# Six check reductions, one tile's split and six small additions change their place in a fused attention and two-layer kernel

## The chip, the cores and the metric

One core of a Trainium2 chip runs the whole program. The engines are the tensor engine (PE in the profile; PEld are its weight loads), VectorE (DVE), ScalarE (ACT), GpSimd (POOL) and SyncE (SP, here only an issuer of DMAs). The time is the device time of one execution in microseconds; the number compared is the median of several executions.

## The reference

Three stages follow one another. The first is attention with 4 batches, 8 heads, 768 positions and heads of 64, in which each position sees the first `n_global` positions and the `n_local` last ones, with a bias that falls with the distance:

```
scores = scale * q @ k.T - slope[h] * dist       # kept where global or local, else -1e9
a = exp(scores - max);  a = a / (sum(a) + 1e-9)
x = (a @ v), as 3072 rows of 512
h = x @ w_in;  x2 = (h * sigmoid(h)) @ w_out     # 512 -> 2048 -> 512
logits = x2 @ phi                                # 32 slots
d = softmax over the rows;  slot_input = d.T @ x2
slot_out[e] = relu(slot_input[e] @ w1[e]) @ w2[e]
out = softmax over the slots(logits) @ slot_out
```

## The kernel before

The 3072 rows are 24 tiles of 128 (six for each batch, `TPB`), and the tiles make 8 chunks of three. Everything lies in one hand-laid arena in SBUF, so most operands in the profile are called `arena`; PSUM is eight banks.

*Attention.* For each tile T: `load` brings q, k and v (for tiles 6 and up into the staging buffers `stage_m`, so that the next load waits until the tile before has been split), `split` makes a high and a low half in 16 bits (`hi`, L200, L202 or L204 by engine, and `lo`, L208 or L210), `s_step` computes the scores of two heads (matmuls L317 or L327, then on VectorE L332 adds the bias and takes the extreme, on ScalarE L333 takes the exponential and adds up the row sums into `psum_`), and `pv_step` multiplies by v (matmuls L372) and divides by the row sums: an addition of 1e-9 (L383), a reciprocal (L384) and the scaling of the rows (L385). The tiles 0 to 5 are called paired: their q and k are used as they are loaded.

*The two layers.* For each chunk `l1_step(c, f)` runs 12 matmuls (L504 to L506) for each of 16 blocks of 128 columns, then the gating: tanh on ScalarE (L508), a product on VectorE (L510, its instruction is appended to the list `gated`), the high half on ScalarE (L200) and the low half on VectorE (L210). Its outputs rotate through four banks. `l2_part` and `l2_end` do the second layer (L524 to L526) and its output's halves, which SyncE transposes (L537).

*The weights.* They arrive as 16 parts of 64-bit words and are converted in the kernel by `conv`: an unpacking on ScalarE (L462), a mask on VectorE (L464), a check of the masked bits by two matmuls (L469), a shift on VectorE (L472), the high half on ScalarE (L482) and the low half, the second part, on VectorE (L490). Part p's L490 must be done before the second layer's matmuls that use its low half. Parts 8 to 15 are those of the second layer; the last of them are converted during the second layer of the first chunk.

*The checks.* `absmax` (L213) takes the largest magnitude of a sample of some halves, and L895 the largest of the odd bits found by the weight checks; all of them are looked at near the end of the kernel, where a flag decides whether a slower program runs.

*The order.* The text interleaves: while a chunk runs through its layers, the attention items of the next chunks are called between the steps, so many a step, in a list made by `other_items`. What each engine executes is ordered afterwards by a scheduler that goes by its own estimate of when an instruction's operands are ready; the order of the text is its preference. `tc.issue_after(ins)` makes the instructions of its block on the engine of `ins` queue behind `ins`.

Of the kernel before, what the change touches and what calls it, by code (L numbers as in the profile page):

```python
# [12 lines left out]
ALU = mybir.AluOpType  # L13
AX = mybir.AxisListType
# [18 lines left out]
CHUNKS = [3, 3, 3, 3, 3, 3, 3, 3]  # L33
# [12 lines left out]
def p2(e):  # L46
    return float(2.0 ** e)
# [53 lines left out]
def fast_kernel(tc, keepp, q_l, k_l, v_l, q_f, k_f, n_global, n_local, w_in, w_out, phi, w1, w2, shapes, pick_c, out):  # L101
# [8 lines left out]
    with ExitStack() as ctx:  # L110
# [101 lines left out]
        def absmax(col, in_, axis=AX.X):  # L212
            V.tensor_reduce(out=smp[:, col:col + 1], in_=in_, axis=axis, op=ALU.max, apply_absolute_value=True)  # L213
# [39 lines left out]
        def paired(T):  # L253

            return T < NPAIR
# [104 lines left out]
        def pv_step(T, half):  # L360
            t, u = T % TPB, T % NR
            ptb = pt[half]
            if t == 0:
                ptb = ptb.rearrange("p z h s c -> p (z h s) c")[:, 0:8].rearrange("p (z h s) c -> p z h s c", z=2, h=4)
            o = bPV.rearrange("p (h d) -> p h d", h=H)
            blocks = ((0, u),) if t == 0 else ((0, u - 1), (1, u)) if u > 0 else ((0, 0), (1, NR - 1))
            for hh in range(4):
                h = 4 * half + hh
                n = 0
                for s, slot in blocks:  # L370
                    for z, y in ((0, 0), (0, 1), (1, 0)):
                        mm(o[:, h], ptb[:, z, hh, s], v16[:, slot, h, y], start=(n == 0), stop=(n == 3 * len(blocks) - 1))  # L372
                        n += 1
            if half == 1:
                if 1 <= t < TPB - 1:
                    if paired(T):
                        V.tensor_copy(out=v16[0:8, u], in_=vg[0:8])
                    else:
                        hi("P", v16[0:8, u], vg[0:8], 0)
                if t == TPB - 2 and T + 2 < NTILE:  # L380
                    hi("P", vg[0:8], v16[0:8, (T + 2) % NR], 0)
                ri = rinv[T % 2]
                V.tensor_scalar(out=ri, in0=psum_[T % 2], scalar1=1e-9, scalar2=None, op0=ALU.add)  # L383
                V.reciprocal(out=ri, in_=ri)  # L384
                V.tensor_tensor(out=x1f, in0=o, in1=ri.rearrange("p (h o) -> p h o", o=1).to_broadcast([128, H, D]), op=ALU.mult)  # L385
                xb = x16[T % 2]
                x1v = x1f.rearrange("p h d -> p (h d)")
                c, i = chunk_of[T]
                xv = xt[c][:, :, :, 128 * i:128 * i + 128]
                if T < C0 and XTE[T] != "D":  # L390
                    flip(xv[:, 0], xv[:, 1], x1v, XTE[T])
                else:
                    hi(CFG["xhi"], xb[:, 0], x1v, 0)
                    lo("V" if paired(T) else CFG["xlo"], xb[:, 1], x1v, 0, xb[:, 0])
                    nc.sync.dma_start_transpose(out=xv.rearrange("p z c t -> p (z c) t"), in_=xb.rearrange("p z f -> p (z f)"))

        def first_items():
# [15 lines left out]
            items.append(lambda: load(C0 + 1, stage_m))  # L413
            return items

        def other_items():
            items, mark = [], {}
            for T in range(C0, NTILE):
                items.append(lambda T=T: s_step(T, 0))
                if T > C0:  # L420
                    items.append(lambda T=T: pv_step(T - 1, 0))
                items.append(lambda T=T: s_step(T, 1))
                if T + 1 < NTILE:
                    items.append(lambda T=T: split(T + 1))
                if T + 2 < NTILE and not paired(T + 2):
                    items.append(lambda T=T: load(T + 2, stage_m))
                items.append(lambda T=T: s_step(T, 2))
                if T > C0:
                    items.append(lambda T=T: pv_step(T - 1, 1))
                    mark[T - 1] = len(items)  # L430
                items.append(lambda T=T: s_step(T, 3))
                if paired(T + 2):
                    items.append(lambda T=T: load(T + 2, None))
            items.append(lambda: pv_step(NTILE - 1, 0))
            items.append(lambda: pv_step(NTILE - 1, 1))
            mark[NTILE - 1] = len(items)
            return items, [0] + [mark[first[c] + CHUNKS[c] - 1] for c in range(1, NCH)]
# [10 lines left out]
        def w_ahead():  # L448
            while nload[0] < most[0] and holder.get(place[nload[0]]) is None and (GATE.get(nload[0]) is None or GATE[nload[0]] in done_p):
                p = nload[0]  # L450
                holder[place[p]] = p
                nc.sync.dma_start(out=ar.view(place[p], [2048], I32), in_=(w_in if p < 8 else w_out)[p % 8].bitcast(I32))
                nload[0] += 1

        def conv(p):
            assert holder[place[p]] == p
            st = ar.view(place[p], [1024, 2], I32)
            low, high = st[:, :, 0], st[:, :, 1]
            by = ar.view(place[p], [2048], I32).bitcast(U8).rearrange("p (n e) -> p n e", e=8)
            u16 = ar.view(place[p], [2048], I32).bitcast(U16).rearrange("p (n e) -> p n e", e=4)  # L460

            A.activation(out=low, in_=by[:, :, 3], func=AF.Copy, scale=1.0 / 32, bias=-0.484375)  # L462

            V.tensor_scalar(out=u16[:, :, 1], in0=u16[:, :, 3], scalar1=0xF000, scalar2=0x3000, op0=ALU.bitwise_and, op1=ALU.bitwise_xor)  # L464

            zb = u16[:, :, 1].bitcast(BF16)
            for j in range(2):
                g = 32 * (2 * (p % 2) + j)
                mm(bM[g:g + 32], wz, zb[:, 512 * j:512 * j + 512], start=True, stop=True, tile_position=(0, g))  # L469
            if p % 2 == 1:  # L470
                A.activation(out=odd16, in_=bM, func=AF.Abs, accum_out=oddp[:, p // 2:p // 2 + 1])
            V.scalar_tensor_tensor(out=low, in0=high, scalar=3, in1=low, op0=ALU.logical_shift_left, op1=ALU.bitwise_xor)  # L472
            lowf = ar.view(place[p], [1024, 2], F32)[:, :, 0]
            if p < 8:
                dst = [wih[:, z, :, 256 * p:256 * p + 256] for z in range(2)]
                src = lowf.rearrange("p (k f) -> p k f", k=4)
                e = E_WI
            else:
                dst = [woh[:, 2 * (p - 8):2 * (p - 8) + 2, z] for z in range(2)]
                src = lowf.rearrange("p (k f) -> p k f", k=2)  # L480
                e = E_WO
            A.activation(out=dst[0], in_=src, func=AF.Copy, scale=-p2(e - 128))  # L482
            if LOE[p] != "V":
                if LOE[p] == "P":
                    A.activation(out=src, in_=src, func=AF.Copy, scale=-p2(e - 128))
                else:
                    G.tensor_scalar(out=src, in0=src, scalar1=-p2(e - 128), scalar2=0.0, op0=ALU.mult, op1=ALU.add)
                G.tensor_tensor(out=dst[1], in0=src, in1=dst[0], op=ALU.subtract)
            else:
                V.scalar_tensor_tensor(out=dst[1], in0=src, scalar=-p2(e - 128), in1=dst[0], op0=ALU.mult, op1=ALU.subtract)  # L490
            holder[place[p]] = None
            w_ahead()


# [33 lines left out]
        def l2_end(c, m):  # L528
            op = bW[(turn[0] + m) % 4]
            T = first[c] + m  # L530
            xh, xtr = x2hl[m], x2t[T % 3]
            hi("A", xh[:, 0], op, E_X2 - E_G - E_WO)
            lo("V", xh[:, 1], op, E_X2 - E_G - E_WO, xh[:, 0])
            if m == 0:
                absmax(6 + 2 * c, xh[:, 0, 0:128])
                absmax(7 + 2 * c, g_of[CHUNKS[c]][:, 15, 0, 0:128])
            nc.sync.dma_start_transpose(out=xtr, in_=xh.rearrange("p z f -> p (z f)"))  # L537
            at(8 if c == 0 else CFG["lag_l"], lambda: logits(c, m))
# [302 lines left out]
        for c in range(NCH):  # L841
# [11 lines left out]
                    st["d"] += 1  # L853

            for f in range(16):
                if c == 0 and f in (3, 5, 7, 9, 11):
                    most[0] += 1
                    w_ahead()
# [24 lines left out]
            if c == 0:  # L883
# [8 lines left out]
                    if f % 4 == 2:  # L892
                        slot_end()

                V.tensor_reduce(out=odd, in_=oddp, axis=AX.X, op=ALU.max)  # L895
                G.memset(acc, 0.0)
                G.memset(ssum, 0.0)
                G.memset(mrun[0], -3e38)
                absmax(4, wih[:, 0, 0, 0:128])
                absmax(5, woh[:, 0, 0, 0:128])  # L900
                absmax(NSMP - 1, phi16[:, :, 0], AX.XY)
                for m in range(n):
                    l2_end(c, m)
                    tick()
# [493 lines left out]
```

## Time and profile before

| | |
|---|---|
| median of three runs | 718.78 us (715.6 to 720.92) |
| the profiled execution | 712.24 us, its span 710.4 us |
| busy, of the span | PE 93%, PEld 54%, DVE 70%, ACT 51%, POOL 33% |
| busy, us | PE 662.8, DVE 498.2, ACT 362.2, POOL 235.2 |
| mean granted clock of the tensor engine | 0.98 of full speed |

A busy tensor engine isn't one at its peak: its matmuls are pipelined, and the rows of a matmul show about twice the distance from one to the next. The profile's columns are: start, duration, engine, line, operation, output and input by name, count, and in brackets how long the engine stood idle before it and what released it.

### The profile page before, as it was taken

Reading aid. Unit: us, or ns where it says so; the run is one execution under the profiler, and the core shown is the slowest. Engines: PE = TensorE matmul, PEld = TensorE weight load, DVE = VectorE, ACT = ScalarE, POOL = GpSimd, SP = SyncE. Lnnn points to the kernel's source line nnn. Section 1 sums busy time; section 2 is a strip of 40 time slices with the busy share of each in tenths; the row PEclk is TensorE's granted clock in tenths of the full one; section 3 lists DMA queues with packets and bytes.
Section 4 is the critical chain, followed back from the end, with each engine's and each line's share of the span. In section 5 each row is a group of like instructions: output and inputs, shape, how many; then the busy total and the mean of one; then the engine's idle time right before and its main releaser. Section 6 shows DMA issues by size and latency. Waiting matters only on the chain.

```text
span 710.4 us, 13667 instructions
## 1 busy us (share of the span) xinstructions
PE 662.8 (93%) x5175; PEld 384.9 (54%) x5175; DVE 498.2 (70%) x1193; ACT 362.2 (51%) x910; POOL 235.2 (33%) x201
## 2 busy tenths in 40 slices
PE   4569989899999999999999999999999999999992
PEld 3345543356555655566556655665566545664552
DVE  5998999988745876487638773876386158797432
ACT  5768977556423552355235532652266147574322
POOL 4010001134643656254625562356143400260000
PEclk9959999999999999999999999999999999999997
DMA  8998874774572569426735665365425791296998
GB/s 228 244 318 257 245 189 144 199 181 99 118 146 70 105 132 189 96 47 120 166 73 107 146 160 97 80 117 114 75 43 66 208 340 61 96 372 236 380 404 295
DMA packets 165257, 120.08 MB, mean 169 GB/s; under 512 B 143936, under 2 KB 150464, under 8 KB 159168
## 3 DMA queue, kind: packets, MB, share of 16 engines
q1 hardware_dynamic: 163968, 118.15, 63.5%
q10 hardware_dynamic: 1216, 0.99, 0.4%
q8 instruction: 42, 0.69, 0.4%
q14 instruction: 31, 0.25, 0.1%
HBM read 79.01 MB, written 6.29 MB: 120 GB/s over the span
## 4 chain that ended last, share of the span: by engine, by line


## 5 line engine op out<-in xcount | busy, mean ns | idle before, releaser
L202 POOL TENSOR_SCALAR arena<-arena 128x1024 f16<-128x1024 f32 (+3 forms) x107 | 106.4, 1005 | 296.1 <-ACT arena L333 100.5
L504 PE MATMUL bank<-rows,arena 128*128 128x384 f16 x512 | 167.4, 328 | 1.3 <-ACT rows L200 0.7
L506 PE MATMUL bank<-rows,arena 128*128 128x384 f16 x512 | 167.3, 327 | 0.0
L505 PE MATMUL bank<-rows,arena 128*128 128x384 f16 x512 | 167.3, 327 | 0.0
L200 ACT ACTIVATE arena<-bank 128x384 f16<-128x384 f32 (+1 forms) x153 | 77.0, 503 | 151.4 <-DVE bank L510 86.8
L333 ACT ACTIVATE arena<-arena 128x256 f32<-128x256 f32 (+1 forms) x192 | 92.3, 482 | 86.3 <-DVE arena L332 85.0
L525 PE MATMUL bank<-arena 128*128 128x512 f16 x336 | 128.0, 381 | 0.6 <-DVE arena L490 0.5
L526 PE MATMUL bank<-arena 128*128 128x512 f16 x336 | 127.9, 381 | 0.0
L524 PE MATMUL bank<-arena 128*128 128x512 f16 x336 | 126.3, 380 | 0.0
L210 DVE SCALAR_TENSOR_TENSOR arena<-bank,arena 128x384 f16<-128x384 f32 (+2 forms) x154 | 87.8, 570 | 29.9 <-ACT arena L200 29.1
L208 POOL TENSOR_TENSOR arena<-arena 128x1024 f16<-128x1024 f32 (+1 forms) x43 | 89.3, 2078 | 22.9 <-ACT arena L200 20.1
L332 DVE CUSTOM_DVE_ANT_0 arena<-bank,arena 128x256 f32<-128x256 f32 (+1 forms) x192 | 69.8, 395 | 28.9 <-PE bank L327 27.8
L510 DVE SCALAR_TENSOR_TENSOR bank<-arena,bank 128x384 f32<-128x384 f32 x128 | 71.5, 559 | 25.3 <-ACT arena L508 24.5
L208 DVE TENSOR_TENSOR arena<-arena 128x1024 f16<-128x1024 f32 (+2 forms) x52 | 69.4, 1334 | 11.0 <-POOL arena L202 8.8
L210 DVE SCALAR_TENSOR_TENSOR arena<-arena 128x1024 f16<-128x1024 f32 (+3 forms) x64 | 64.2, 1018 | 10.1 <-POOL arena L202 5.6
L200 ACT ACTIVATE arena<-arena 128x1024 f16<-128x1024 f32 (+1 forms) x69 | 61.7, 904 | 15.0 <-DVE arena L210 8.7
L506 PEld LDWEIGHTS <-arena 128*128 128x128 f16 x512 | 50.2, 98 | 33.9 <-issue 1.0
L504 PEld LDWEIGHTS <-arena 128*128 128x128 f16 x512 | 50.3, 98 | 32.1 <-issue 4.3
L508 ACT ACTIVATE arena<-bank 128x384 f32<-128x384 f32 x128 | 61.4, 480 | 9.6 <-PE bank L506 9.2
L505 PEld LDWEIGHTS <-arena 128*128 128x128 f16 x512 | 50.2, 98 | 29.3 <-issue 1.8
L526 PEld LDWEIGHTS <-arena 128*128 128x128 f16 x336 | 32.9, 98 | 40.7 <-issue 2.1
L524 PEld LDWEIGHTS <-arena 128*128 128x128 f16 x336 | 32.8, 98 | 35.5 <-issue 1.8
(185 smaller groups left out, 808.1 us busy)
## 6 DMA issues: line engine op xcount, KB each, us to landing
arena<-in_w_dram SPq DMA_DIRECT2D x31, 1024.0 KB, 7.7
arena<-in_q_l_dram SPq DMA_DIRECT2D x18, 512.0 KB, 3.9
arena<-in_k_l_dram SPq DMA_DIRECT2D x18, 512.0 KB, 4.3
arena<-in_w_in_dram SPq DMA_DIRECT2D x8, 1024.0 KB, 6.1
arena<-in_w_out_dram SPq DMA_DIRECT2D x8, 1024.0 KB, 5.9
arena<-in_v_l_dram SPq DMA_DIRECT2D x24, 256.0 KB, 3.1
out_dram<-arena SPq DMA_DIRECT2D x4, 768.0 KB, 8.5
arena<-in_q_f_dram SPq DMA_DIRECT2D x6, 256.0 KB, 5.3
```

The source lines that it names most:

```text
L200: A.activation(out=out, in_=in_, func=AF.Copy, scale=p2(e))
L202: G.tensor_scalar(out=out, in0=in_, scalar1=p2(e), scalar2=0.0, op0=ALU.mult, op1=ALU.add)
L208: (V if eng == "V" else G).tensor_tensor(out=out, in0=in_, in1=h, op=ALU.subtract)
L210: return V.scalar_tensor_tensor(out=out, in0=in_, scalar=p2(e), in1=h, op0=ALU.mult, op1=ALU.subtract)
L333: A.activation(out=pw, in_=pw, func=AF.Exp, scale=-1.0, bias=nmx[:, T, h:h + 1], accum_out=psum_[T % 2][:, h:h + 1])
L504: mm(hp, wh, x[:, 0, k], start=(k == 0), stop=False)
L505: mm(hp, wh, x[:, 1, k], start=False, stop=False)
L506: mm(hp, wl, x[:, 0, k], start=False, stop=(k == 3))
L510: gated.append(V.scalar_tensor_tensor(out=hp, in0=th, scalar=1.0, in1=hp, op0=ALU.add, op1=ALU.mult))
L524: mm(op, gh, woh[:, f, 0], start=(f == 0), stop=False)
L525: mm(op, gh, woh[:, f, 1], start=False, stop=False)
L526: mm(op, gl, woh[:, f, 0], start=False, stop=(f == 15))
```

## The change

The addition of 1e-9 to the row sums of the tiles 0 to 5 is done by GpSimd (as a multiplication by 1 and an addition) in place of VectorE. The VectorE instructions of tile 8's split are queued behind the second part of the last weight conversion. Six reductions for the checks, which stood in the text behind the first chunk's second layer, are called in the second chunk, at its fifth block, and queued behind the product of its fourth.

```
@@ pv_step
                 ri = rinv[T % 2]
-                V.tensor_scalar(out=ri, in0=psum_[T % 2], scalar1=1e-9, scalar2=None, op0=ALU.add)
+                if paired(T):
+                    G.tensor_scalar(out=ri, in0=psum_[T % 2], scalar1=1.0, scalar2=1e-9, op0=ALU.mult, op1=ALU.add)
+                else:
+                    V.tensor_scalar(out=ri, in0=psum_[T % 2], scalar1=1e-9, scalar2=None, op0=ALU.add)
                 V.reciprocal(out=ri, in_=ri)
@@ new function
+        def split_behind(T):
+            assert nconv == 16
+            with tc.issue_after(parted[0].ins):
+                split(T)
@@ other_items
-                    items.append(lambda T=T: split(T + 1))
+                    items.append(lambda T=T: split(T + 1) if T != 7 else split_behind(T + 1))
@@ conv
+        parted = [None]
...
-                V.scalar_tensor_tensor(out=dst[1], in0=src, scalar=-p2(e - 128), in1=dst[0], op0=ALU.mult, op1=ALU.subtract)
+                parted[0] = V.scalar_tensor_tensor(out=dst[1], in0=src, scalar=-p2(e - 128), in1=dst[0], op0=ALU.mult, op1=ALU.subtract)
@@ l2_end
-            if m == 0:
+            if m == 0 and c:
                 absmax(6 + 2 * c, xh[:, 0, 0:128])
                 absmax(7 + 2 * c, g_of[CHUNKS[c]][:, 15, 0, 0:128])
@@ the loop over the chunks
             for f in range(16):
+                if c == 1 and f == 4:
+                    with tc.issue_after(gated[-1].ins):
+                        V.tensor_reduce(out=odd, in_=oddp, axis=AX.X, op=ALU.max)
+                        absmax(6, x2hl[0][:, 0, 0:128])
+                        absmax(7, g_of[CHUNKS[0]][:, 15, 0, 0:128])
+                        absmax(4, wih[:, 0, 0, 0:128])
+                        absmax(5, woh[:, 0, 0, 0:128])
+                        absmax(NSMP - 1, phi16[:, :, 0], AX.XY)
...
-                V.tensor_reduce(out=odd, in_=oddp, axis=AX.X, op=ALU.max)
                 G.memset(acc, 0.0)
                 G.memset(ssum, 0.0)
                 G.memset(mrun[0], -3e38)
-                absmax(4, wih[:, 0, 0, 0:128])
-                absmax(5, woh[:, 0, 0, 0:128])
-                absmax(NSMP - 1, phi16[:, :, 0], AX.XY)
```

## Rows read from the trace of the kernel before

**Rows 1.** Waits of PE, 146 to 580 us: total, times, longest.

```profile
PE bank L372 <- DMA arena<-arena: 0.7, 1, 0.7
```

**Rows 2.** Waits of PE, 98 to 146 us.

```profile
PE bank L469 <- DVE arena L464: 2.6, 4, 0.8
PE bank L317 <- DVE arena L332: 2.1, 1, 2.1
PE bank L469 <- DVE arena L384: 0.6, 1, 0.6
```

**Rows 3.** Busy time by stretch: PE, PEld, DVE, ACT, POOL, granted clock, DMA.

```profile
98.00:143.50 45.50, 39.65 (x238) 17.42 (x237) 44.04 (x71) 28.18 (x55) 5.15 (x4) 0.96 0.63 180
...
150.00:165.00 15.00, 15.00 (x137) 9.91 (x135) 12.75 (x43) 10.76 (x35) 3.63 (x3) 1.00 0.69 154
```

**Rows 4.** Timeline of DVE, parts of 54 to 152 us.

```profile
54.25 0.45 DVE L213 TENSOR_REDUCE arena<-arena 128x1 f32<-128x128 f16 x2
55.12 1.32 DVE L464 TENSOR_SCALAR arena<-arena 128x1024 uint16<-128x1024 uint16 x1 [0.43 <-ACT arena L462]
...
111.38 2.17 DVE L472 SCALAR_TENSOR_TENSOR arena<-arena 128x1024 int32<-128x1024 int32 x1
...
135.47 0.17 DVE L383 TENSOR_SCALAR arena<-arena 128x8 f32<-128x8 f32 x1
135.54 1.31 DVE L464 TENSOR_SCALAR arena<-arena 128x1024 uint16<-128x1024 uint16 x1
...
136.74 0.24 DVE L213 TENSOR_REDUCE arena<-arena 128x1 f32<-128x128 f16 x1
...
139.75 1.21 DVE L472 SCALAR_TENSOR_TENSOR arena<-arena 128x1024 int32<-128x1024 int32 x1
...
140.96 0.27 DVE L213 TENSOR_REDUCE arena<-arena 128x1 f32<-128x128 f16 x1
141.15 1.21 DVE L208 TENSOR_TENSOR arena<-arena 128x1024 f16<-128x1024 f32 x1
142.28 1.21 DVE L490 SCALAR_TENSOR_TENSOR arena<-arena 128x1024 f16<-128x1024 f32 x1
...
151.75 0.56 DVE L210 SCALAR_TENSOR_TENSOR arena<-bank,arena 128x384 f16<-128x384 f32 x1
```

**Rows 5.** Timeline of PE, parts of 143 to 156 us.

```profile
143.35 0.33 PE L504 MATMUL bank<-rows,arena 128*128 128x384 f16 x1
143.55 0.38 PE L525 MATMUL bank<-arena 128*128 128x512 f16 x1
...
155.81 0.33 PE L504 MATMUL bank<-rows,arena 128*128 128x384 f16 x1
155.97 0.33 PE L505 MATMUL bank<-rows,arena 128*128 128x384 f16 x1
```

**Rows 6.** L383 on DVE, 16 to 136 us: busy us, mean ns.

```profile
L383 DVE TENSOR_SCALAR arena<-arena 128x8 f32<-128x8 f32 x6 | 1.1, 182 | 0.0
```

**Rows 7.** POOL: line L357 (ns min/median/max, starts), and its timeline.

```profile
L357 POOL TENSOR_SCALAR arena<-arena x6: 190/380/1101, 15.1 to 45.1; 128x1 f32<-128x1 f16 x6
...
110.35 2.12 POOL L202 TENSOR_SCALAR arena<-arena 8x1024 f16<-8x1024 f16 x1 [8.91 <-DVE arena L383]
136.55 2.74 POOL L202 TENSOR_SCALAR arena<-arena 128x1024 f16<-128x1024 f32 x2 [24.08 <-DMA arena<-in_k_l_dram]
```

**Rows 8.** Timeline of ACT, two instructions.

```profile
119.94 0.19 ACT L333 ACTIVATION_READ_ACCUMULATOR arena<-arena 128x1 f32 x1
...
141.00 1.15 ACT L482 ACTIVATE arena<-arena 128x1024 f16<-128x1024 f32 x1 [2.23 <-DVE arena L472]
```

**Rows 9.** Timeline of SP's queue, 142 to 149 us.

```profile
142.39 0.33 SPq L268 DMA_DIRECT2D arena<-in_k_l_dram  x1
...
146.17 2.62 SPq L537 DMA_TRANSPOSE arena<-arena  x2
```

**Rows 10.** Busy time, columns as in rows 3.

```profile
100.00:120.00 20.00, 16.65 (x88) 6.71 (x86) 19.38 (x29) 12.58 (x24) 2.42 (x2) 0.91 0.52 156
```

## The prediction

> **What bounds the kernel now.** I read the page's busy times first (the table above): the tensor engine is busy for 93% of the span, so time can only be won where it stands still or runs slowly. The list of its waits comes next, cut in two at 146 us. Behind the cut, up to 580 us, it waits once, for 0.7 us [rows 1]; work that leaves or joins VectorE there is free as long as the tensor engine doesn't come to wait for it. Ahead of the cut, from 98 us, its waits add up to 5.3 us in the three rows shown, all of them for VectorE [rows 2]. The table by stages [rows 3] says why: between 98 and 143.5 us VectorE is busy for 44.04 of 45.5 us, the tensor engine for 39.65. This is the second layer of the first chunk, in which the last weight parts are still being converted. So VectorE sets the pace until the last conversion ends, the tensor engine does so from then on, and the change works just at the seam. The last question is therefore which instructions stand ahead of the sixteenth conversion's second part (L490 at 142.28 us, ending at 143.49) and when the tensor engine takes it up (L525 at 143.55) [rows 4, 5].
>
> **Part 1, six additions to GpSimd.** Tiles 0 to 5 each lose one L383 on VectorE, 182 ns of busy time on average [rows 6]. Neighbouring instructions overlap, so what one costs in a dense stretch is read from start to start: tile 5's starts at 135.47 and its successor at 135.54, so 0.07 us [rows 4]. The six together are bounded by 6 x 0.182 = 1.1 us; only tile 5's stands in the dense chain that I could follow back from the seam. On GpSimd there is no such addition to read; the nearest rows are six gate instructions of 128x1, 0.19 us at best and 1.10 at worst [rows 7]. I take 0.2 us, the best row, since where an addition takes longer its cover is far longer still. For a wait is added: the reciprocal L384 on VectorE now waits for GpSimd. Behind it on VectorE stand the row scaling L385, and after that the next conversion parts, for which the tensor engine waits. Tile 5's sums are complete when ScalarE has read its last accumulator, at 119.94 + 0.19 = 120.13 us [rows 8]; its reciprocal stood behind the L464 of 135.54 [rows 4], and GpSimd is idle for the 24.08 us before 136.55 [rows 7]. So the wait is covered by some 16 us. If GpSimd took up tile 8's first scalings ahead of the addition, that cover would be gone; that is a rival below.
>
> A price from the other side belongs here: a GpSimd instruction can hold VectorE up. The copy of 8x1024 at 110.35 ran to 112.47 [rows 7], and the conversion step L472 that began under it at 111.38 took 2.17 us, where the same step at 139.75 took 1.21 [rows 4]. A small addition can do this for its own length only: 6 x 0.2 = 1.2 us is the upper end of the cost. The Trainium skill, in "SBUF — State Buffer", section "Who interferes with whom", states as a rule that VectorE and GpSimd share one pair of ports, held for a whole instruction by whichever came first, and that a VectorE instruction with two SBUF inputs counts among those that need it while a GpSimd instruction reads SBUF; the 2.17 us agree with it, and it speaks against this part. By the rule alone the part would cost up to that 1.2 us and give back less.
>
> **Part 2, tile 8's split behind L490.** Only VectorE's four instructions of the split get the new order (its scalings on GpSimd don't): the low half of k, of v, the maximum, the low half of q. Of these just one stood ahead of L490: L208 128x1024 at 141.15, 1.21 us, from start to start 142.28 - 141.15 = 1.13 us [rows 4]. But L490 also needs ScalarE's high half, which runs from 141.00 for 1.15 us, to 142.15 [rows 8]. With the low half of k out of the way L490 can start at about 142.18 instead of 142.28: 0.1 us. The other 1.03 us turn into idle time of VectorE, and the wait for ScalarE is what is late next.
> What is moved brings a load along: the k of tile 9 goes into the same staging buffer, and SyncE issued it at 142.39, right behind the low half of k [rows 9]. That half now ends at about 144.4, so the load is issued 2.0 us later. Behind it in SyncE's queue stand the load of v and the transposes of the second layer's output, which began at 146.17 as soon as VectorE had written that output [rows 9]; the issues of k and v, 0.33 us each, fit before that. GpSimd's scaling of k for tile 9 comes 2 us later, as does its low half on VectorE, with the gating steps L510 behind it. For these the cover is the four banks: the bank of chunk 1's f = 0 is free when L210 at 151.75 is done (0.56 us, 152.31) [rows 4] and is taken again at 155.81 [rows 5], so 3.5 us are in hand. I cost it at nothing; without that cover it would be up to 2.0 us.
>
> **Part 3, maxima into the second chunk.** Six reductions are moved: the odd-bits one (L895), three maxima over the weights, two over the first chunk (all L213). Two ran at 54.25 (0.45 us together) in front of a wait of 0.43 us for ScalarE's unpacking of the next weights, and so were free; one stood at 136.74, L895 and one more directly ahead of 141.15 (0.19 us from 140.96 to there, and L895 is no longer), and the last ran behind L490 [rows 4]. L895 and its neighbour fall into the time in which L490 waits for ScalarE anyway, so only the one at 136.74 counts, at the same 0.19 us. In chunk 1 the six stand behind L510 of f = 3: 6 x 0.19 = 1.1 us of VectorE at most, in a stretch in which it is busy for 12.75 of 15 us [rows 3] while the tensor engine doesn't wait [rows 1]. The four banks cover it with the same 3.5 us; without them it would be the 1.1.
>
> **The sum at the seam.** VectorE's side: 0.07 + 0.19 + 0.1 = 0.36 us earlier. The tensor engine's side: L525 stands behind the L504 at 143.35; from one such matmul to the next it is 0.16 us (155.81 to 155.97), so it could have started at 143.51 without VectorE, 0.04 us sooner [rows 5]; and its own last stop ahead of that, 0.6 us for the check of the sixteenth conversion [rows 2], which waits for the L464 behind L383, is shortened by L383's 0.07. So it gains 0.04 + 0.07 = 0.11 us, the smaller of the two, and the rest is left over. From there on it runs without a stop. Bounds: if all VectorE time taken ahead of the seam were on the path, 1.1 + 0.45 + 3 x 0.19 + 1.13 = 3.25 us would be won; if the additions hold VectorE up for their full length and nothing is won, 1.2 us are lost. I take -0.1, since both sides of the seam have rows and they agree within 0.3 us. The profiled execution took 712.24 us (span 710.4 and 1.84 around it); it becomes 712.1. The median of the three runs shown is 718.78, 0.9% longer, between 715.6 and 720.92; I carry the same 0.1 over, to 718.7. One per cent, 7.2 us, is about what a measurement of this kernel can tell from no change.
>
> **The rivals.**
> A. The order is made anew and the worst stop goes. The engines' order isn't the order of the text: two maxima that the text has behind the second layer ran at 54.25 [rows 4]. Moving ten VectorE instructions and six additions may place others differently too. The dearest accident of the present order is the scores' wait for L332, 2.1 us, with the longest stop for a check, 0.8 us, just ahead of it [rows 2], and a granted clock of 0.91 over the 20 us around it, so 0.09 x 20 = 1.8 us [rows 10]. All gone: -4.7, 714.1. For it: VectorE is nearly saturated there, so small shifts decide. Against: of the edits only tile 3's addition lies shortly ahead of it. 0.14.
> B. The same accident the other way: one more stop of that kind with its fall of the clock, between 98 and 143.5 us: +4.7, 723.5. It decides from the point at which a conversion's check stands at the head of the tensor engine's queue with VectorE a whole conversion step behind. 0.10.
> C. The addition of tile 5 lands behind tile 8's scalings on GpSimd, at 136.55 for 2.74 us [rows 7]. It would be done at about 139.5, the reciprocal at the head of VectorE would wait from the end of the L464 on, about 136.7, and the last two conversions with it: +2.8, 721.6. It needs GpSimd's queue to have the addition behind the scalings; its inputs, 16 us earlier, speak against it. 0.08.
> D. GpSimd's additions hold VectorE up in the dense stretch: +1.2, 719.9, by the row of 2.17 us against 1.21. The VectorE steps beside them are conversion steps like that one, which speaks for it; the length of 0.2 us, which may fall into a gap, against. 0.10. This is what the page named above makes a rule.
> E. The edits don't do what they say, because the order had things there already or brings them back: 718.8. 0.10, and the time alone doesn't tell it from the forecast.
>
> **How the numbers follow.** The forecast has 0.48. Forecast, D and E lie between -0.1 and +1.2, with bounds of -3.25 and +1.2; C gives 721.6, A and B 714.1 and 723.5. To hold 8 in 10 the range takes in those bounds, C, D and A, leaves out B, and allows for a median that may lie anywhere in the middle of 715.6 to 720.92 by the spread of the runs: 714.0 to 723.0. No case reaches 7.2 us by itself; A and B with the spread of the runs on top might, so faster 0.04, within 1% 0.92, slower 0.04.
>
> **What would show it.** Right: no L383 on VectorE for the first six tiles, and six GpSimd instructions of about 0.2 us in their place; the sixteenth L490 starting straight behind ScalarE's high half, the low half of k for tile 8 behind it; six reductions behind chunk 1's fourth L510; the tensor engine's waits between 98 and 146 us within half a microsecond of today's, and none worth naming from 146 to 580. Wrong: a reciprocal whose releaser is GpSimd, with more than a few tenths; a tensor engine that waits for L210 or L510 in chunk 1; a new wait or another fall of the clock ahead of 143 us, which would mean that the order, and not the edits, made the time.

## The result and the profile after

The changed kernel takes 719.63 us in the median of 20 runs (713.85 to 723.46), the kernel before 715.44 in 20 runs (711.64 to 720.92): a ratio of 1.0055 [1.0033, 1.0078], slower by about 4 us. The forecast was no change. The kernel before was read as 718.78 from three runs; two of those three are the highest of its twenty, while its profiled execution, at 712.24, lies at the lower end. The profiled execution of the changed kernel took 718.89 us (span 717.1), so the two profiles lie 6.7 us apart where the medians lie 4.2 apart.

To find where the 6.7 us arise I compared the first tanh of each chunk (ScalarE, L518 now). Chunk 0 begins at 53.77 us (before 55.65), chunk 1 at 154.25 (before 148.77): chunk 0 took 100.48 us in place of 93.12. Chunk 1 then took 72.78 (before 72.94), and behind the last tanh come 93.7 us (before 93.2). So 5.5 of the 6.7 us are there when the second chunk begins. The length of chunk 0 overstates this, because its start moves too: in the profiles of this document it lies anywhere from 51.67 to 57.24 us. So I also count from a stop that all of them have, the scores' wait for L332, to chunk 1's first tanh: the matmul behind that wait (L317) starts at 107.25 us before and at 107.68 now, and chunk 1 begins 41.5 us later before and 46.6 now. So 5.1 us arise behind that stop. I read first what the tensor engine waited for; this view answers to [rows 2], and its second part, from 146 to 588 us, to [rows 1]:

```profile
PE bank L479 <- DVE arena L474: 5.6, 5, 3.3
PE bank L317 <- DVE arena L332: 2.1, 1, 2.1
PE bank L534 <- DVE arena L210: 0.9, 1, 0.9
PE bank L535 <- DVE arena L500: 0.4, 1, 0.4
...
PE bank L372 <- DMA arena<-arena: 0.9, 1, 0.9
PE bank L556 <- DMA arena<-arena: 0.4, 2, 0.2
```

The waits ahead of 146 us add up to 9.0 us, against 5.8 before: the 5.3 of [rows 2] and a fourth row of the same view,

```profile
PE bank L525 <- DVE arena L490: 0.5, 1, 0.5
```

The wait for L332 is as long as it was. New are a stop of 0.9 us for L210, ahead of that wait, and one of 3.3 us for a conversion's check (L479, before L469), behind it. The windows (columns as in [rows 3]) show what follows on it:

```profile
98.00:146.00 48.00, 38.96 (x225) 16.54 (x224) 43.33 (x66) 28.20 (x59) 8.56 (x6) 0.89 0.71 179
100.00:120.00 20.00, 15.99 (x100) 6.47 (x98) 17.68 (x25) 10.73 (x19) 2.72 (x2) 0.83 0.48 139
...
138.00:142.00 4.00, 0.77 (x3) 0.32 (x4) 2.13 (x2) 3.30 (x7) 0.78 (x1) 0.92 0.72 232
142.00:146.00 4.00, 4.00 (x13) 1.52 (x12) 4.00 (x6) 2.77 (x9) 2.68 (x2) 0.65 0.01 4
146.00:150.00 4.00, 4.00 (x21) 1.81 (x19) 3.92 (x5) 0.90 (x2) 0.00 (x0) 1.00 0.90 134
...
150.00:165.00 15.00, 15.00 (x110) 9.21 (x109) 11.54 (x34) 7.74 (x21) 2.80 (x4) 1.00 0.72 193
```

The tensor engine is busy for 0.77 of the 4 us from 138, and in the 4 us behind that its granted clock is 0.65 on average, between its two levels (1.2 and 2.4 GHz, 0.5 and 1.0 here), before it is back at 1.00. The stop costs 3.3 us and the clock behind it 0.35 x 4 = 1.4 us, 4.7 together. Over the whole 48 us the clock is 0.89, against 0.96 in [rows 3]; from 100 to 120 us it is 0.83, against 0.91 in [rows 10].

Why the check was late is read backwards, from the tensor engine to VectorE, ScalarE and SyncE. First the timeline of the tensor engine in the changed kernel:

```profile
141.23 0.61 PE L479 MATMUL bank<-arena 128*32 128x512 bf16 x2 [3.28 <-DVE arena L474]
```

VectorE's timeline of the same kernel:

```profile
122.18 2.48 DVE L208 TENSOR_TENSOR arena<-arena 64x1024 f16<-64x1024 f32 x2
124.58 1.22 DVE L482 SCALAR_TENSOR_TENSOR arena<-arena 128x1024 int32<-128x1024 int32 x1
...
126.13 1.31 DVE L474 TENSOR_SCALAR arena<-arena 128x1024 uint16<-128x1024 uint16 x1
127.24 1.26 DVE L208 TENSOR_TENSOR arena<-arena 128x1024 f16<-128x1024 f32 x1
128.41 1.22 DVE L500 SCALAR_TENSOR_TENSOR arena<-arena 128x1024 f16<-128x1024 f32 x1
...
139.87 1.31 DVE L474 TENSOR_SCALAR arena<-arena 128x1024 uint16<-128x1024 uint16 x1 [2.26 <-ACT arena L472]
...
145.40 1.23 DVE L500 SCALAR_TENSOR_TENSOR arena<-arena 128x1024 f16<-128x1024 f32 x1
```

ScalarE's:

```profile
138.70 1.14 ACT L472 ACTIVATE arena<-arena 128x1024 int32<-128x1024 uint8 x1 [6.15 <-DMA arena<-in_w_out_dram]
```

and that of SyncE's queue:

```profile
127.71 0.57 SPq L268 DMA_DIRECT2D arena<-in_q_l_dram  x1
129.69 0.33 SPq L460 DMA_DIRECT2D arena<-in_w_out_dram  x1
```

The check's mask (L474 at 139.87) stood at the head of VectorE, which was idle for 2.26 us until ScalarE had unpacked the last weight part (L472 at 138.70); ScalarE had waited 6.15 us for that part's load. The load uses the staging buffer of part 12, which is free after part 12's second part, L500 at 128.41. In the kernel before, the same places read, on VectorE:

```profile
121.28 1.23 DVE L472 SCALAR_TENSOR_TENSOR arena<-arena 128x1024 int32<-128x1024 int32 x1 [0.39 <-PE bank L469]
...
123.76 1.22 DVE L490 SCALAR_TENSOR_TENSOR arena<-arena 128x1024 f16<-128x1024 f32 x1
...
126.44 1.95 DVE L208 TENSOR_TENSOR arena<-arena 64x1024 f16<-64x1024 f32 x2
```

on SyncE's queue and on ScalarE:

```profile
126.83 0.52 SPq L452 DMA_DIRECT2D arena<-in_w_out_dram  x1
...
129.75 0.57 SPq L268 DMA_DIRECT2D arena<-in_q_l_dram  x1
```

```profile
132.12 1.16 ACT L462 ACTIVATE arena<-arena 128x1024 int32<-128x1024 uint8 x1 [1.41 <-DMA arena<-in_w_out_dram]
```

Before, part 12's second part ran at 123.76 and the load was issued at 126.83, ahead of tile 8's q (129.75), and was unpacked at 132.12. Now the q load goes first, at 127.71, the weight part at 129.69, and it is unpacked 9.0 us later instead of 5.3. So it is issued 2.9 us later and is 3.7 us longer under way.

And why did part 12 end 4.65 us later? VectorE's order is another one: two low halves of 64x1024, one of them of tile 7's q (L208 at 122.18, 2.48 us), now stand ahead of part 12's shift (L482 at 124.58), and a mask of part 13 and a low half of 128x1024 (126.13, 127.24) ahead of its second part. None of these is an instruction that the change touches.

The edits themselves did what they say. The six additions run on GpSimd, 18 are left on VectorE, and the six reductions stand in chunk 1; the group of POOL's L384 in the changed kernel (ns min/median/max, first and last start; it answers to [rows 7]):

```profile
L384 POOL TENSOR_SCALAR arena<-arena x6: 204/309/945, 16.0 to 121.4; 128x8 f32<-128x8 f32 x6
```

and VectorE's timeline in its chunk 1:

```profile
163.28 0.15 DVE L868 TENSOR_REDUCE arena<-arena 128x1 f32<-128x8 f32 x1
163.35 1.05 DVE L213 TENSOR_REDUCE arena<-arena 128x1 f32<-128x128 f16 x5
```

### The profile page after: what moved, and what is told of

The parts are those of the page before. It is cut to its first block, busy times and chain, and to the rows that moved or that the text cites. A ratio compares the mean times of both kernels' runs of the same rounds, so it can differ in the third digit from the quotient of the medians.

```text
span 717.1 us, 13672 instructions
## 1 busy us (share of the span) xinstructions
PE 667.6 (93%) x5175; PEld 385.7 (54%) x5175; DVE 498.1 (69%) x1187; ACT 362.1 (50%) x910; POOL 241.8 (34%) x207
## 4 chain that ended last, share of the span: by engine, by line
## 5 line engine op out<-in xcount | busy, mean ns | idle before, releaser
L210 DVE SCALAR_TENSOR_TENSOR arena<-bank,arena 128x384 f16<-128x384 f32 (+2 forms) x154 | 87.8, 571 | 28.9 <-ACT arena L200 28.0
L208 POOL TENSOR_TENSOR arena<-arena 128x1024 f16<-128x1024 f32 (+1 forms) x43 | 89.4, 2080 | 23.1 <-ACT arena L200 20.3
L332 DVE CUSTOM_DVE_ANT_0 arena<-bank,arena 128x256 f32<-128x256 f32 (+1 forms) x192 | 70.0, 395 | 29.7 <-PE bank L327 27.7
L520 DVE SCALAR_TENSOR_TENSOR bank<-arena,bank 128x384 f32<-128x384 f32 x128 | 71.0, 557 | 26.2 <-ACT arena L518 25.4
L208 DVE TENSOR_TENSOR arena<-arena 128x1024 f16<-128x1024 f32 (+2 forms) x52 | 69.5, 1336 | 11.6 <-POOL arena L202 10.8
L210 DVE SCALAR_TENSOR_TENSOR arena<-arena 128x1024 f16<-128x1024 f32 (+3 forms) x64 | 64.2, 1018 | 10.9 <-POOL arena L202 6.0
L518 ACT ACTIVATE arena<-bank 128x384 f32<-128x384 f32 x128 | 61.6, 481 | 13.6 <-PE bank L516 13.1
```

The lines of the kernel that those rows point to most:

```text
L208: (V if eng == "V" else G).tensor_tensor(out=out, in0=in_, in1=h, op=ALU.subtract)
L210: return V.scalar_tensor_tensor(out=out, in0=in_, scalar=p2(e), in1=h, op0=ALU.mult, op1=ALU.subtract)
L520: gated.append(V.scalar_tensor_tensor(out=hp, in0=th, scalar=1.0, in1=hp, op0=ALU.add, op1=ALU.mult))
```

## The experiments

The first theory: the time went into the engines' order, which is made anew for the whole program, by way of part 12 and the late load. Its rivals: GpSimd's additions cost the time themselves (waits for them, or VectorE held up); or the split and the maxima do. Each ratio is to the kernel before on the same chip, with its 95% interval (12 runs of each kernel, 6 of the additions alone and of the additions left out); starts and stops come from one profiled execution each, so tenths of a microsecond in them are not weighed.

**The additions alone.**

```
-                V.tensor_scalar(out=ri, in0=psum_[T % 2], scalar1=1e-9, scalar2=None, op0=ALU.add)
+                if paired(T):
+                    G.tensor_scalar(out=ri, in0=psum_[T % 2], scalar1=1.0, scalar2=1e-9, op0=ALU.mult, op1=ALU.add)
+                else:
+                    V.tensor_scalar(out=ri, in0=psum_[T % 2], scalar1=1e-9, scalar2=None, op0=ALU.add)
```

> Only the six additions go to GpSimd; split and maxima stay as before. Theory 1 (order: the additions make the scheduler order VectorE anew, so that the twelfth-index conversion's second part and with it the load of the last weight part come late): slower than before by 3 to 7 us, a ratio of 1.004 to 1.010, with the last weight part's load issued behind tile 8's q and a stop of the tensor engine of over 2 us for the last check, as in the changed kernel. Theory 2 (the additions themselves hold VectorE up or make reciprocals wait): the same time, but then the loss lies beside the GpSimd additions and not at the last check. Theory 3 (the moved split and maxima load the second chunk): 0.999 to 1.001.

1.0071 [1.0046, 1.0096], 720.19 us. This part alone loses as much as the whole. But the long stop that I looked for isn't there. The last weight part's load is issued behind tile 8's q as expected (127.87 and 125.94), but the last check stops the tensor engine for 1.3 us only; chunk 1 begins at 148.97, about as in the profile before (148.77), though from the wait for L332 on it takes 42.9 us, 1.4 more. Chunk 1 then takes 75.1 us, 2.2 more than before, and 3.2 us more arise behind it. The tensor engine's waits behind 146 us:

```profile
PE bank L372 <- DMA arena<-arena: 2.6, 1, 2.6
PE bank L549 <- DVE arena L552: 2.2, 1, 2.2
```

L549 is the logits' matmul of the first chunk, L552 VectorE's read of the logits before it. In the kernel before, that read ends at 159.35 us and the next logits start at 159.93 without a wait.

**The split and the maxima alone** (the diff of the change without its first part).

> The additions stay on VectorE; tile 8's split and the six reductions are moved as in the change. Theory 1: no loss, 0.997 to 1.001, and the last weight part's load is issued ahead of tile 8's q as before. Theory 2: the same, 0.997 to 1.001. Theory 3: the whole loss, 1.004 to 1.007, with the tensor engine waiting for the gating in the second chunk.

1.0031 [1.0004, 1.0059], 716.68 us: a small loss, against what I expected, and a doubtful one, since one of the twelve runs took 725.38 us and the medians alone are 1.0015 apart. The check of the last part stops the tensor engine for 0.6 us, as before; chunk 1 begins at 150.59, and its logits stop the engine for 1.3 us.

**The changed kernel with tile 7's split behind part 12's second part**, on VectorE.

```
-            with tc.issue_after(parted[0].ins):
+            with tc.issue_after(part[12 if T == 7 else 15].ins):
...
-                    items.append(lambda T=T: split(T + 1) if T != 7 else split_behind(T + 1))
+                    items.append(lambda T=T: split(T + 1) if T not in (6, 7) else split_behind(T + 1))
```

> The changed kernel with one thing more: VectorE's part of tile 7's split is queued behind the second part of the conversion of weight part 12, whose staging buffer the last part's load needs. Additions, tile 8's split and maxima stay as changed. Theory 1: the loss is gone, 0.997 to 1.002 of before, the last weight part lands some 5 us after its issue at about 126 us, and the stop for the last check is under 1 us. Theory 2: the loss stays, 1.004 to 1.007. Theory 3: the loss stays, 1.004 to 1.007.

1.0047 [1.0022, 1.0072], 718.41 us. The seam came back for the most part: part 12's second part at 124.4, chunk 1's first tanh at 149.98 (43.7 us from the wait for L332, where the changed kernel has 46.6), no stop for a check above 1.0 us. The time did not, so the theory was not enough: chunk 1 took 76.3 us. VectorE's timeline in it:

```profile
156.14 1.22 DVE L208 TENSOR_TENSOR arena<-arena 128x1024 f16<-128x1024 f32 x1 [3.13 <-POOL arena L202]
...
161.02 1.05 DVE L213 TENSOR_REDUCE arena<-arena 128x1 f32<-128x128 f16 x5
```

GpSimd's:

```profile
155.06 1.04 POOL L202 TENSOR_SCALAR arena<-arena 128x1024 f16<-128x1024 f32 x1 [12.51 <-DMA arena<-in_k_l_dram]
```

that of SyncE's queue:

```profile
150.82 0.57 SPq L268 DMA_DIRECT2D arena<-in_k_l_dram  x1
```

and the tensor engine's:

```profile
162.91 0.38 PE L555 MATMUL bank<-arena 128*128 128x64 f16 x8 [2.21 <-DVE arena L558]
```

The k of tile 9 is loaded at 150.82, where [rows 9] have 142.39. GpSimd's scaling waits for it, VectorE stands 3.13 us at the low half behind the scaling, with the reads of the logits queued behind that low half and then behind the reductions. The logits of all tiles go through one bank, so the next logits' matmul waits for the read of the last. From here on the theory had a second place: the one bank between two logits, with 159.93 - 159.35 = 0.58 us of cover in the kernel before.

**The kernel before with the last weight part's load queued behind tile 8's q load**, and nothing else.

```
-            holder[place[p]] = None
-            w_ahead()
+            if p != 12:
+                holder[place[p]] = None
+                w_ahead()
...
+        def load_last():
+            load(8, stage_m)
+            holder[place[12]] = None
+            with tc.issue_after(loaded[8].ins):
+                w_ahead()
...
-                    items.append(lambda T=T: load(T + 2, stage_m))
+                    items.append(lambda T=T: load(T + 2, stage_m) if T != 6 else load_last())
```

> The kernel before with no part of the change; only the load of the last weight part is queued behind tile 8's q load. Theory 1: slower by 2 to 5 us, 1.003 to 1.007, with a stop of the tensor engine of 2 us or more for the last check and an unpacking that waits for the load. Theory 2 and theory 3: 0.999 to 1.001, since neither the additions nor the moved work are in it.

1.0035 [1.0012, 1.0058], 718.18 us. This edit loses time, and chunk 1 begins at 153.04, 4.3 us later than before. But 3.1 of these are there already at the end of the wait for L332 (110.36), over 22 us before the load is issued (132.91), so the trace doesn't show that the load's place makes the loss; this edit, too, has the order made anew. The single long stop that I expected isn't there: the stops for checks are five of at most 0.8 us, though the load takes 7.1 us to its unpacking.

**The changed kernel with tile 9's split behind the first chunk's last logits**, the maxima moved from f = 4 to f = 11.

```
-            with tc.issue_after(parted[0].ins):
+            with tc.issue_after((seen[2] if T == 9 else parted[0]).ins):
...
-                if c == 1 and f == 4:
+                if c == 1 and f == 11:
```

> The changed kernel; VectorE's part of tile 9's split is queued behind the first chunk's last logits, and the six reductions are called at the twelfth block of the second chunk in place of the fifth, behind the logits. Theory 1 (in the changed kernel the loss is made at the seam by the late last weight part; in the runs without that it is made in the second chunk, where one bank between two logits gives only 0.6 us of cover): the loss stays, 1.003 to 1.007, with the stop for the last check of 2 us or more, and no stop in the second chunk. Theory 3 (the moved split and maxima load the second chunk and make the loss of the changed kernel): 0.998 to 1.002.

1.0042 [1.0014, 1.007], 718.87 us. No stop for VectorE at the logits, and the loss stays: the check's stop is 3.2 us, chunk 1 begins at 153.86. In the changed kernel the seam alone holds the loss.

**Both repairs**, on VectorE's order alone: tile 7's split behind part 12, tile 9's behind the logits, maxima at f = 11. All six additions stay on GpSimd.

> The repair of the run before last (tile 7's split behind the conversion of part 12) and the one of the run just named together; additions on GpSimd, tile 8's split as changed. Theory 1: both places repaired, so no loss, 0.997 to 1.002; no stop for logits in the second chunk (2.2 us with the first repair alone), stops for checks under 1 us each. Theory 2 (the additions on GpSimd cost the time themselves): 1.004 to 1.007 still.

1.0009 [0.9986, 1.0031], 715.88 us: no loss is left that these runs could tell. The tensor engine's waits ahead of 146 us have no long stop for a check:

```profile
PE bank L478 <- DVE arena L473: 2.1, 4, 1.0
PE bank L317 <- DVE arena L332: 2.1, 1, 2.1
```

VectorE's timeline has part 12's shift and second part ahead of the two low halves of 64x1024, not behind them:

```profile
121.32 1.23 DVE L481 SCALAR_TENSOR_TENSOR arena<-arena 128x1024 int32<-128x1024 int32 x1 [0.26 <-PE bank L478]
...
123.81 1.22 DVE L499 SCALAR_TENSOR_TENSOR arena<-arena 128x1024 f16<-128x1024 f32 x1
...
126.49 1.94 DVE L208 TENSOR_TENSOR arena<-arena 64x1024 f16<-64x1024 f32 x2
```

**The split alone, and the maxima alone.** The diffs are those parts of the change.

> Only tile 8's split is moved; additions and maxima as before. Theory 1: the k of tile 9 is loaded 2 to 4 us later, VectorE waits 0.5 to 1.5 us for GpSimd's scaling of it, and the tensor engine's stop for the logits is that less 0.6 us: 0 to 0.9 us; in time 1.000 to 1.002. Theory 3, with all of the loss in this part: 1.004 to 1.006.

> Only the six reductions are moved. Theory 1: they stand directly ahead of the first chunk's first logits on VectorE for 1.1 us, and the tensor engine's stop there is 1.1 less 0.6, 0.3 to 0.7 us; in time 0.999 to 1.002. Theory 3, with all of the loss in this part: 1.004 to 1.006.

1.0003 [0.9983, 1.0023] and 1.001 [0.9989, 1.0031]; 716.56 and 716.74 us. Neither can be told from no change. In their traces the logits' matmul waits 1.0 us with the split (k of tile 9 loaded at 146.58, 4.2 us later than in [rows 9], of which 2.1 are the later start of chunk 1, 150.85) and 0.7 us with the maxima, at the upper ends of what I had worked out from the 0.58 us of cover or just above.

**The additions of the six tiles left out**, and no instruction given to GpSimd.

```
-                V.tensor_scalar(out=ri, in0=psum_[T % 2], scalar1=1e-9, scalar2=None, op0=ALU.add)
-                V.reciprocal(out=ri, in_=ri)
+                if paired(T):
+                    V.reciprocal(out=ri, in_=psum_[T % 2])
+                else:
+                    V.tensor_scalar(out=ri, in0=psum_[T % 2], scalar1=1e-9, scalar2=None, op0=ALU.add)
+                    V.reciprocal(out=ri, in_=ri)
```

> The kernel before, with the addition of 1e-9 left out for the tiles 0 to 5 (the reciprocal takes the sums as they are); no GpSimd instruction is added, split and maxima stay. Less work than before on every engine. Theory 1 (the gap that the additions leave on VectorE makes the order anew): slower than before all the same, 1.003 to 1.008, with the twelfth-index conversion's second part behind tile 7's split. Theory 2 (the additions on GpSimd cost the time): 0.998 to 1.001.

1.0084 [1.0053, 1.0115], 721.61 us. Six instructions less than before, none in their place, and the slowest kernel of the study. Here no addition on GpSimd can be blamed. VectorE's timeline:

```profile
121.17 2.48 DVE L208 TENSOR_TENSOR arena<-arena 64x1024 f16<-64x1024 f32 x2
123.57 1.23 DVE L475 SCALAR_TENSOR_TENSOR arena<-arena 128x1024 int32<-128x1024 int32 x1
...
127.42 1.23 DVE L493 SCALAR_TENSOR_TENSOR arena<-arena 128x1024 f16<-128x1024 f32 x1
```

and the tensor engine's in chunk 1:

```profile
162.54 0.38 PE L549 MATMUL bank<-arena 128*128 128x64 f16 x8 [2.14 <-DVE arena L552]
```

Around part 12 it is the order of the changed kernel, with the two low halves ahead of part 12's shift and its second part at 127.42. The loss lies elsewhere, though: the last check stops the tensor engine for 0.8 us, and the logits of chunk 1 for 2.1.

**Four of the six additions on GpSimd**, and then **one**.

```
-                V.tensor_scalar(out=ri, in0=psum_[T % 2], scalar1=1e-9, scalar2=None, op0=ALU.add)
+                if T in (0, 1, 2, 5):
+                    G.tensor_scalar(out=ri, in0=psum_[T % 2], scalar1=1.0, scalar2=1e-9, op0=ALU.mult, op1=ALU.add)
...
```

(in the other kernel `if T in (4,):`)

> Four of the six additions go to GpSimd, those of the tiles 0, 1, 2 and 5; split and maxima stay. VectorE keeps its order of before around the last conversions. Theory 1: 0.998 to 1.002. Theory 2: two thirds of the loss, 1.003 to 1.005.

> One addition goes to GpSimd, tile 4's, an instruction of 0.15 us that starts 0.06 us ahead of its successor; split and maxima stay. VectorE's order around the last conversions is that of the changed kernel. Theory 1: 1.003 to 1.008 for this one instruction. Theory 2: at most a sixth of the loss, 1.000 to 1.002.

Four: 0.9976 [0.9952, 1.0001], 715.27 us. One: 1.0054 [1.0029, 1.0078], 719.61 us. Four moved instructions lose nothing, one loses as much as the whole change. VectorE's timeline with the four:

```profile
118.50 1.23 DVE L475 SCALAR_TENSOR_TENSOR arena<-arena 128x1024 int32<-128x1024 int32 x1 [0.38 <-PE bank L472]
...
120.99 1.22 DVE L493 SCALAR_TENSOR_TENSOR arena<-arena 128x1024 f16<-128x1024 f32 x1
...
123.68 1.95 DVE L208 TENSOR_TENSOR arena<-arena 64x1024 f16<-64x1024 f32 x2
```

and with the one:

```profile
121.92 2.48 DVE L208 TENSOR_TENSOR arena<-arena 64x1024 f16<-64x1024 f32 x2
124.32 1.22 DVE L475 SCALAR_TENSOR_TENSOR arena<-arena 128x1024 int32<-128x1024 int32 x1
...
128.15 1.22 DVE L493 SCALAR_TENSOR_TENSOR arena<-arena 128x1024 f16<-128x1024 f32 x1
```

With the four, part 12's second part (120.99) runs before the two low halves (123.68); with the one, it is the other way round. The last check then stops the tensor engine for 1.0 us, not 3.3. Tile 4's addition stands in the dense stretch of the kernel before:

```profile
110.20 0.15 DVE L383 TENSOR_SCALAR arena<-arena 128x8 f32<-128x8 f32 x1
```

In the profile of the four the granted clock from 100 to 120 us is 1.00, where [rows 10] have 0.91. The interval of the four still touches 1.

**The changed kernel with tile 8's loads behind the last weight part's load** on SyncE.

```
+        def load_behind(T):
+            with tc.issue_after(wload[15].ins):
+                load(T, stage_m)
...
-                    items.append(lambda T=T: load(T + 2, stage_m))
+                    items.append(lambda T=T: load(T + 2, stage_m) if T != 6 else load_behind(T + 2))
```

> The changed kernel; the loads of tile 8 are queued on SyncE behind the load of the last weight part, VectorE's order of the conversions stays. It parts the two ways in which that load is late: issued late (129.7 against 126.8 us, since its buffer comes free late) and long under way (9.0 against 5.3 us, beside tile 8's q and the transposes). If the q load beside it makes the long way: landing after about 6 us, the stop for the last check down from 3.3 to about 0.5 us, in time 1.001 to 1.004. If the late issue is what counts: the stop stays above 2 us, 1.004 to 1.007.

1.0025 [1.0004, 1.0047], 718.49 us. The load is issued at 131.03, still late, and unpacked at 136.68: 5.6 us from issue, not 9.0. The last check's stop falls from 3.3 to 0.1 us, chunk 1 begins at 152.02, and its logits then stop the tensor engine for 1.7 us. By the ratios about half of the loss goes (1.0055 to 1.0025, with intervals that overlap).

**Where the time goes in each kernel**, in us, from the profiles: from the end of the wait for L332 to chunk 1's first tanh; the stop for the last check; the last weight part's load, from issue to unpacking; chunk 1; the longest stop for logits in it.

| kernel | to chunk 1 | last check | load | chunk 1 | logits |
|---|---|---|---|---|---|
| before | 41.5 | 0.6 | 5.3 | 72.9 | none |
| changed | 46.6 | 3.3 | 9.0 | 72.8 | none |
| additions alone | 42.9 | 1.3 | 6.8 | 75.1 | 2.2 |
| additions left out | 42.8 | 0.8 | 6.2 | 76.7 | 2.1 |
| tile 4's addition | 43.8 | 1.0 | 6.4 | 73.8 | 0.8 |
| four additions | 41.7 | 0.4 | 5.5 | 73.5 | 0.4 |
| late load | 42.7 | 0.5 | 7.1 | 73.5 | 0.3 |
| tile 7's split behind part 12 | 43.7 | under 0.1 | 6.1 | 76.3 | 2.2 |
| tile 9's split behind the logits | 46.6 | 3.2 | 8.9 | 72.8 | none |
| both repairs | 42.7 | under 0.1 | 6.1 | 72.3 | none |
| tile 8's loads behind the last part's | 43.4 | 0.1 | 5.6 | 74.6 | 1.7 |

The long stop and a load of 9 us occur in two kernels only, together. The additions alone, the additions left out and tile 4's addition have the changed kernel's order around part 12 and on SyncE's queue, with the q load 1.1 to 1.9 us ahead, and there the load takes 6.2 to 6.8 us. So that order makes the load late; what makes it 2 to 3 us longer still in the changed kernel, no run shows.

## Why the prediction was wrong

**The step that failed first** is the one in the sum: "I take -0.1, since both sides of the seam have rows and they agree within 0.3 us". Both sides had rows of the old order. The sum priced each edit inside that order: tile 5's addition at 0.07 us, the others at their busy time at most. What the edits cost is the order that is made anew: moving one addition, tile 4's, an instruction of tenths of a microsecond that part 1 priced only within the bound for all six, lost 0.54%; taking out all six and giving nothing to GpSimd lost 0.84%; moving four lost nothing; and all six with VectorE's order put right at the seam and at the logits gave 1.0009. The order is therefore shown to be the cause, and GpSimd's additions are shown not to be. In the changed kernel the cost of that order is the late load and the stop of 3.3 us for the last check; in the kernels with one addition moved or none left, which have the same order around part 12, a loss as large lies in other places.

**Rival B was the case that came**, at a chance of 0.10: one more long stop for a check with a fall of the clock, 3.3 + 1.4 = 4.7 us in the profile. That this is the very price it was given is luck, since that price had other parts (2.1, 0.8 and 1.8). The prediction's own sign that the order made the time, a new wait or another fall of the clock ahead of 143 us, is there. What set off the stop was another thing. VectorE wasn't "a whole conversion step behind"; it stood idle for 2.26 us, and what was late was a load, whose buffer VectorE had freed 4.65 us later than before, some 12 us ahead of the stop's end (129.6 and 141.2). I had looked for the order's sensitivity next to the edits ("of the edits only tile 3's addition lies shortly ahead of it"), and gave A, the same accident for the better, the larger chance. The kernels with no addition and with one moved show that neither an edit close by nor an added instruction is needed.

**The cover of "the four banks"** in parts 2 and 3 was the wrong cover. For the products of chunk 1 the 3.5 us held: no wait for L210 or L520 is among the tensor engine's in its chunk 1. But VectorE's queue also carries the reads of the logits, and behind them stands one bank with 0.58 us. Split and maxima together stop the tensor engine there for 1.3 us, singly for 1.0 and 0.7. I had "up to 2.0" and "1.1" as the price without cover, which was the right size for the wrong place. In the changed kernel itself this place costs nothing: its chunk 1 takes no longer than before.

**What was right.** No reciprocal came to wait for GpSimd, so C didn't happen; the additions took 0.20 to 0.94 us, 0.31 in the median, against the 0.2 that I took from [rows 7]; D's hold of VectorE didn't decide, since the four additions cost nothing; the reductions run behind chunk 1's fourth product; and from 146 us on the tensor engine sets the pace. That the absolute time lies in the range owes much to the three runs of before, which were high as a median; the 4 us of the change itself were missed.

**What stays open.** In the kernels of the additions alone and of none, the tensor engine also waits 2.6 and 3.0 us for a transposing DMA (L372) late in the kernel, [rows 1] having 0.7; no run tested why. Why the load takes 9 us in the changed kernel and 6 to 7 in others with the same order of loads is open. The edit that makes the load late in the kernel before lost 0.35% without the long stop, and I can't say in which form. Whether four additions on GpSimd are a real gain of 0.24% or none was not settled. Why the order puts the two low halves ahead of part 12 is open; that it does so when tile 4's addition leaves is what the traces show.

## What to carry to other kernels

Where the order of the engines is worked out for the whole program, compare the order of before and after first, far from the edit too, and ask which buffer each displaced instruction frees and which load waits for it; the price of an edit read inside the old order holds only if that order stays. A part that is "off the path" needs the cover of every reader in the same queue, the narrowest bank among them, not of the one that the edit is about. And one instruction added or left out, without any wait, is a cheap trial of how much of a measured difference order alone can make: here as much as the whole change.

## What was not expected of the hardware

The same load, the last weight part, took 5.3 to 6.1 us from issue to the unpacking that waited for it where tile 8's q load stands behind it on SyncE's queue, in the kernel before and in seven others, one of which issues it late (131.03 us, 5.6). In the six kernels with the q load 1.1 to 2.1 us ahead of it, it took 6.2 to 9.0. So the neighbour on the queue, and not the late issue, goes with a longer load; it rests on one execution of each kernel, the two groups nearly touch, and the 9 us themselves are not explained by it. And a GpSimd scaling held a VectorE conversion step again: the second part at 132.97 us took 2.18 us beside a GpSimd scaling of 1.99 us that began at 132.09, where the other second parts shown took 1.22 or 1.23. That agrees with the rule of the Trainium skill in "SBUF — State Buffer", section "Who interferes with whom", as [rows 7] and [rows 4] did; the small additions, 0.31 us in the median, showed no loss by it.
